# The end of the ramp: the last stage's rows in one area, loaded by six DMAs; the second batch's first product between the `pd` groups; the rounding of weights reordered

## The chip, the cores and the metric

The kernel runs on one core of one Trainium2 chip. A core has five engines that run their own streams of instructions: TensorE (PE) multiplies matrices, VectorE (DVE), ScalarE (ACT) and GpSimd (POOL) work on tensors elementwise, and SyncE (SP) issues DMAs. ScalarE and GpSimd can issue DMAs too. Engines wait for each other and for DMAs through semaphores. Operands lie in SBUF (128 partitions), products in PSUM (eight banks of 128 x 512 fp32). The metric is the time of one execution in microseconds; lower is better.

## The reference

A Fourier filter over the sequence, then a two-layer network with SiLU on every token:

```python
# x (8, 3008, 256), filt_r and filt_i (1505, 256)
X = np.fft.rfft(x, axis=1)
y = np.fft.irfft(X * (filt_r + 1j * filt_i)[None], n=x.shape[1], axis=1)
# t = y reshaped to (24064, 256); w_in (256, 2048), w_out (2048, 256)
h = t @ w_in
out = (h * (1.0 / (1.0 + np.exp(-h)))) @ w_out
```

The weights arrive as 64-bit floats; the kernel rounds them to fp32 on the chip.

## The kernel before, in words

**Two halves that interleave.** The sequence of 3008 is split as 47 x 64 (in fact 94 x 32 with real arithmetic), so that the Fourier transform becomes small matrix products. For one batch (`spectral(b)`) the stages are: a product over rows (`pa`, `stage1`), a product over the other factor (`pb`, `forward`), the multiplication with the filter (`multiply`, `add`), the inverse product (`pc`, `inverse_first` for batch 0), a pass of the rows through DRAM to change the layout (`rows_first` stores to `d2`, `load_t4` loads from it), and the last product (`pd`, `stage3`), whose result is the input `y` of the network. The network works on pairs of token blocks, 48 steps for each batch; a step (`hidden` and `project`) does seven products into `px` and `pyz`, SiLU into `g`, and seven products into `acc`, with the seven-product (Strassen-like) form of a 2 x 2 block product. That form needs sums of weight blocks, which `combine_weights(jp)` makes for pair `jp` of the eight pairs of 128-column weight blocks.

**The ramp.** Only batch 0 runs ahead of the loop; the other batches' stages are placed between the products of the loop's steps by `plan` and `put(step, round, piece)`. The order is written out by hand: the program records instructions in this order, each engine runs its own in that order, and semaphores do the rest. A piece at `put(k, 7, ...)` is recorded after the last round of step `k`. Tiles come from pools with a fixed number of buffers; asking for one more makes the writer wait for the readers of the oldest. In the ramp PSUM banks are dealt in rotation by `bank` with a counter, `early[0]`; `early[0] = None` ends that.

**The end of the ramp**, which the change touches. For groups `g` = 0 to 5 of eight rows, `inverse_first(g)` fills two banks, and `rows_first(g)` (L515 to L521) copies each to SBUF with ScalarE and stores it to `d2` in DRAM: ScalarE issues the store, but GpSimd for group 4. `rows_first` takes its two tiles from the pools `q` and `o`, two buffers each, so a copy of group 5 waits for the store of group 3. Stage 3 needs all 48 rows of `d2`, for four columns a time. `load_t4(g, first, last)` (L539 to L547) loads rows `first` to `last` of the four columns of group `g`, one DMA for each half `h`, into a tile of its own. Before the change it is called for `g` = 0 to 3 and rows 0 to 24, then 24 to 32, then 32 to 48, when the stores of these rows are on their way: 24 DMAs, of which SP issues 20 and ScalarE the four with `first == 32` and `h == 1`.

While the rows travel, the weight blocks 4 to 8 are turned into fp32: `split` (L922 to L932: VectorE takes exponent and mantissa bits apart, ScalarE turns them into floats), `rounded` (L938 to L944, VectorE) and `placed` (L953, VectorE: the product goes to its place in `w_t`). The exponent of a block goes over two ScalarE pieces (L931, L932) for the blocks 0, 2, 4 and 6 and over one VectorE piece (L940) for the others. `combine_weights` runs on VectorE for pair 0 and on GpSimd for pairs 2 and 3. TensorE runs filler products (`idle_wide`, L1015), whose result nobody reads, and then `stage3` for the groups 0 to 3, each into two banks; between groups stand filler products of 256 columns (L554). The banks are evicted into `y` in turn by VectorE (L244) and ScalarE (L246, and L576 for group 0). Then `tokens` (the `ty` tile, VectorE) starts the loop.

**The first steps of the loop.** In step 0 the second batch's first row product stands between the products of the network (`stage1(0)` of batch 1, `put` at step 0, round 3: the `pa` rows of L333), with two evictions by ScalarE (L349), and the same for `u` = 1 to 7 in steps 1 to 7. In these steps another weight block is split, rounded and placed too.

Of the kernel before, what the change touches and what calls it, by code (L numbers as in the profile page):

```python
# [167 lines left out]
def kernel(  # L168
# [51 lines left out]
    w_t = cpool.tile([128, NJP, 7, 2, 128], FP32)  # L220
    warm = cpool.tile([128, 1], FP32)
    bias_t = cpool.tile([128, 5], FP32)
    x_all = xpool.tile([128, 2, 2, 2 * C], FP32)
# [13 lines left out]

    flip, early = [0], [0]

    def evac(dst, src):  # L240

        flip[0] ^= 1
        if flip[0]:
            nc.vector.tensor_copy(out=dst, in_=src)  # L244
        else:
            nc.scalar.copy(out=dst, in_=src)  # L246

# [19 lines left out]
    def spectral(b):  # L267
# [24 lines left out]

# [27 lines left out]
        def sums(u):  # L320
# [4 lines left out]
            us[u] = ut  # L325

        def stage1(u):
            t1 = tpool.tile([128, 2, 2, C], FP32, name=f"t1_{b}_{u}", tag="t")
            ps = [bank(b, f"pa_{b}_{u}_{h}", HIDDEN[h] if b > 1 and u == 6 else None) for h in range(2)]
            if b == 1:  # L330
                xt = xs.pop(u)
                for h in range(2):
                    nc.tensor.matmul(out=ps[h].rearrange("p n c -> p (n c)"), lhsT=wx_t,  # L333
                                     rhs=xt[0:96, 512 * h:512 * h + 512], start=True, stop=True)
                if u + 2 < 8:
                    load_x(u + 2)
            else:
                ut = us.pop(u)
                for par in range(2):
                    for h in range(2):  # L340
                        rows = slice(64 * h, 64 * h + N1)
                        nc.tensor.matmul(out=ps[h][64 * par:64 * par + 64], lhsT=wf_t[rows, par],  # L342
                                         rhs=ut[rows, par], start=True, stop=True)
# [171 lines left out]
        def rows_first(g):  # L515
            for i, pool, tag in ((0, qpool, "q"), (1, opool, "o")):
                qt = pool.tile([128, 2, C], FP32, name=f"q_{b}_{g}_{i}", tag=tag)
                nc.scalar.copy(out=qt, in_=halves[g][i])
                a0 = 8 * g + 4 * i
                queue = nc.gpsimd if g == NG - 2 else nc.scalar  # L520
                queue.dma_start(out=d2[a0:a0 + 4].rearrange("a n h c -> (a n) h c"), in_=qt)  # L521

# [15 lines left out]

        def load_t4(g, first=0, last=2 * NS):  # L539
            if first == 0 and b == 0 and g in (2, 3):  # L540
                t4s[g] = tpool.tile([128, 4, C], FP32, name=f"t4_{b}_{g}", tag="t")
            elif first == 0:
                t4s[g] = t4pool.tile([128, 4, C], FP32, name=f"t4_{b}_{g}", tag="t4")
            for h in range(2):
                queue = nc.scalar if first == 32 and h == 1 else nc.sync
                queue.dma_start(out=t4s[g][64 * h + first:64 * h + last],
                                in_=d2[first:last, 4 * g:4 * g + 4, h, :])  # L547

        def stage3(g, home=None, fill=()):
# [3 lines left out]
            for moving in fill:  # L553
                nc.tensor.matmul(out=room[0][:, 0], lhsT=wx_t, rhs=moving, start=True, stop=True)  # L554
            ps = [t.rearrange("p a c -> p (a c)")[:, 0:8 * N1]
                  .rearrange("p (a i n) -> p a i n", a=2, i=4) for t in room]
            for cb in range(2):
                for i in range(4):
                    for c0 in (0, 64):
                        for h in range(2):  # L560
                            rows = slice(64 * h, 64 * h + 2 * NS)
                            nc.tensor.matmul(  # L562
                                out=ps[h][c0:c0 + 64, cb, i, :],
                                lhsT=t4s[g][rows, i, 128 * cb + c0:128 * cb + c0 + 64],
                                rhs=wi_t[rows, :], start=True, stop=True)
# [8 lines left out]
            for h in range(2):  # L574
                if g == 0:
                    nc.scalar.copy(out=dst[:, :, h, n0:n0 + 4], in_=ps[h])  # L576
                else:
                    evac(dst[:, :, h, n0:n0 + 4], ps[h])

        def evict_y(g, h):  # L580
# [4 lines left out]

        return dict(evict_y=evict_y, evict_t1=evict_t1, halves=halves, load_first=load_first, stage1_first=stage1_first, load_x=load_x, sums=sums, stage1=stage1, reverse_x=reverse_x,
                    load_fold=load_fold, fold=fold, stage1_fold=stage1_fold, evict_fold=evict_fold,
                    load_t2=load_t2, forward=forward, multiply=multiply, add=add, inverse=inverse, inverse_first=inverse_first, rows_first=rows_first, even=even, rows=rows, load_t4=load_t4, stage3=stage3)

# [319 lines left out]
    def split_weights(*js):  # L909
# [17 lines left out]
        for j in js:  # L927
            if j in (0, 2, 4, 6):

# [5 lines left out]
    def round_weights(*js):  # L935
        for j in js:
            lo, hi, e, m, ef, mf = raws[j]
            v.scalar_tensor_tensor(out=mf, in0=lo, scalar=2.0 ** -52, in1=mf, op0=ALU.mult, op1=ALU.add)  # L938
            if j not in (0, 2, 4, 6):
                v.tensor_scalar(out=e, in0=ef, scalar1=255.0, scalar2=float(1 << 23),  # L940
                                op0=ALU.min, op1=ALU.mult)
# [115 lines left out]
    for g in range(NG):  # L1057
# [10 lines left out]
        if g == 2:  # L1068
# [129 lines left out]
```

## Time and profile before

| | us |
|---|---|
| median of three runs (2581.76 to 2582.83) | 2582.73 |
| the profiled execution | 2582.95 |
| its span, first to last instruction | 2581.1 |
| TensorE busy in the span | 2560.4 |
| VectorE busy | 1679.8 |
| ScalarE busy | 1112.5 |
| GpSimd busy | 424.0 |

In the table of stages, the end of the ramp and the first steps read (busy us in the stretch, mean rate of all DMAs):

| stretch, us | what runs | TensorE | VectorE | ScalarE | GpSimd | GB/s |
|---|---|---|---|---|---|---|
| 36.0 to 62.2 | batch 0 up to the last inverse product | 25.45 | 23.33 | 13.69 | 11.51 | 280 |
| 62.2 to 72.9 | rows through DRAM, filler on TensorE | 9.50 | 10.56 | 6.34 | 4.90 | 189 |
| 72.9 to 80.2 | stage 3, groups 0 to 3, evictions | 7.30 | 5.88 | 3.91 | 3.27 | 34 |
| 80.2 to 88.0 | step 0 | 6.95 | 6.06 | 4.80 | 2.02 | 328 |
| 88.0 to 96.0 | step 1 | 8.00 | 6.25 | 4.29 | 1.97 | 191 |
| 96.0 to 104.0 | step 2 | 8.00 | 6.43 | 4.57 | 1.97 | 185 |

A line of the timeline is read as: start in us from the span's start, duration, engine, line of the kernel, operation, written tile, read tiles, shape, number of merged instructions, and in brackets how long the engine had been idle and what it had waited for. An engine name with q is its sequencer, which issues DMAs. [...] The chain that ended last is followed back from the last instruction, each step to what released it.

### The profile page before, as it was taken

To read this page: it belongs to the slowest core of one execution; us is meant where nothing else is said; L and a number is where in the kernel's file an instruction comes from. 1 tells how busy PE (TensorE), PEld (TensorE's weight loads), DVE (VectorE), ACT (ScalarE), POOL (GpSimd) and SP (SyncE) were. 2 spreads that over 40 slices of the span, in tenths; PEclk is the share of its full clock that TensorE was granted. 3 is DMA by queue.
4 is the path that set the end of the run, shared out by engine and by line. 5 is a ranking of instruction groups with operands and counts; after the bars stand their busy time and mean duration, and the time that the engine had idled before them with its cause. 6 is when DMAs were issued, how large, how long until landed. Compare 5 with 4: busy or idle time off the path is not lost.

```text
span 2581.1 us, 48332 instructions
## 1 busy us (share of the span) xinstructions
PE 2560.4 (99%) x18956; PEld 2197.1 (85%) x18956; DVE 1679.8 (65%) x3569; ACT 1112.5 (43%) x3014; POOL 424.0 (16%) x672
## 2 busy tenths in 40 slices
PE   8999999999999999999999999999999999999998
PEld 6788888888888888888888888888888888888987
DVE  7866666666666666666666666666666666555554
ACT  3544444444444444444444444444444444444443
POOL 2211111121112111311122111211121112101101
PEclk9999999999999999999999999999999999999999
DMA  8531232222222222322223122331232211200000
GB/s 279 156 74 49 72 79 63 60 63 75 60 63 69 70 62 58 77 72 66 61 65 83 50 66 58 80 80 46 66 85 64 69 42 33 58 19 16 9 17 17
DMA packets 200077, 171.08 MB, mean 66 GB/s; under 512 B 122116, under 2 KB 174196, under 8 KB 199060
## 3 DMA queue, kind: packets, MB, share of 16 engines
q1 hardware_dynamic: 178520, 117.04, 18.5%
q0 software_dynamic: 16928, 44.65, 5.4%
q10 hardware_dynamic: 4400, 6.29, 0.8%
q8 instruction: 149, 2.44, 0.4%
q14 instruction: 80, 0.66, 0.1%
HBM read 96.05 MB, written 81.26 MB: 69 GB/s over the span
## 4 chain that ended last, share of the span: by engine, by line
PE 96%; DVE 1%; DMA 1%; ACT 1%; issue 0%; ACTq 0%; POOL 0%; SPq 0%; DVEq 0%; POOLq 0%
PE acc L797 43%; PE px L734 25%; PE pyz L734 19%; PE pd L562 3%; PE pb L446 2%; PE pc L489 2%; PE pf L416 1%; DMA filt<-in_filt_r_dram 1%; DVE g L705 0%; DMA w_t<-in_x_dram 0%; PE pa L342 0%; PE pc L511 0%; PE idle L1015 0%; ACT t L349 0%; ACTq L233 0%
## 5 line engine op out<-in xcount | busy, mean ns | idle before, releaser
L797 PE MATMUL acc<-g,w_t 128*128 128x256 f32 (+1 forms) x5376 | 1509.1, 375 | 0.4 <-DVE g L705 0.4
L797 PEld LDWEIGHTS acc<-g,w_t 128*128 128x128 f32 x5376 | 1021.8, 190 | 115.2 <-DVE g L705 0.8
L705 DVE TENSOR_TENSOR g<-pyz,abc 128x256 f32<-128x256 f32 (+1 forms) x1152 | 479.3, 416 | 613.4 <-ACT abc L755 359.6
L705 DVE TENSOR_TENSOR g<-g 128x256 f32<-128x256 f32 (+3 forms) x1152 | 598.2, 519 | 196.5 <-ACT g L738 183.4
L734 PE MATMUL px<-ty,w_t 128*128 128x256 f32 (+1 forms) x2304 | 677.9, 376 | 0.7 <-ACT abc L755 0.6
L738 ACT ACTIVATE g<-g 128x256 f32<-128x256 f32 (+1 forms) x1152 | 472.9, 410 | 250.0 <-DVE g L705 250.0
L734 PEld LDWEIGHTS px<-ty,w_t 128*128 128x128 f32 x2304 | 432.3, 190 | 64.4 <-issue 7.9
L705 POOL TENSOR_TENSOR s<-s 128x256 f32<-128x256 f32 (+1 forms) x329 | 254.7, 791 | 1412.9 <-DVE s L817 1307.8
L734 PE MATMUL pyz<-y,w_t 128*128 128x256 f32 (+1 forms) x1536 | 453.8, 377 | 0.0
L734 PEld LDWEIGHTS pyz<-y,w_t 128*128 128x128 f32 x1536 | 283.2, 189 | 48.1 <-DVE g L705 8.9
L749 ACT COPY abc<-px 128x256 f32<-128x256 f32 (+1 forms) x384 | 141.1, 368 | 365.2 <-PE px L734 365.2
L755 ACT COPY abc<-px 128x256 f32<-128x256 f32 (+1 forms) x384 | 141.6, 369 | 336.3 <-PE px L734 335.6
L738 ACT ACTIVATE g<-px 128x256 f32<-128x256 f32 (+1 forms) x384 | 145.8, 380 | 297.6 <-PE px L734 297.5
L734 PE MATMUL px<-y,w_t 128*128 128x256 f32 (+1 forms) x768 | 231.9, 384 | 0.1
L734 PE MATMUL pyz<-ty,w_t 128*128 128x256 f32 (+1 forms) x768 | 225.3, 375 | 0.2 <-DVE g L705 0.2
L734 PEld LDWEIGHTS px<-y,w_t 128*128 128x128 f32 x768 | 140.0, 189 | 33.2 <-DVE y L584 5.8
L734 PEld LDWEIGHTS pyz<-ty,w_t 128*128 128x128 f32 x768 | 144.3, 190 | 18.8 <-DVE g L705 1.0
L742 ACT COPY abc<-px 128x256 f32<-128x256 f32 (+1 forms) x384 | 135.4, 353 | 43.7 <-PE px L734 43.7
L562 PEld LDWEIGHTS pd<-wi_t,t 48*64 48x64 f32 x4096 | 65.7, 135 | 28.8 <-ACT g L738 16.4
L428 POOL DMA_DIRECT2D d<-tf x144 | 71.4, 503 | 29.5 <-DVE tf L424 25.4
L817 ACT COPY s<-acc 128x512 f32<-128x512 f32 (+1 forms) x94 | 54.2, 577 | 47.6 <-PE acc L797 47.5
L562 PE MATMUL pd<-wi_t,t 48*64 48x47 f32 x4096 | 72.2, 233 | 2.5 <-issue 2.2
(124 smaller groups left out, 1316.0 us busy)
## 6 DMA issues: line engine op xcount, KB each, us to landing
t<-d SPq DMA_DIRECT2D x120, 192.0 KB
d<-q POOLq DMA_DIRECT2D x86, 256.0 KB, 2.6
t<-d SPq DMA_DIRECT2D x84, 256.0 KB
out_dram<-o SPq DMA_DIRECT2D x636, 32.0 KB
d<-tf POOLq DMA_DIRECT2D x144, 96.0 KB, 3.2
xr<-in_x_dram SPq DMA_DIRECT2D x6, 1472.0 KB
x_all<-in_x_dram SPq DMA_DIRECT2D x72, 96.0 KB
x_all<-xr SPq DMA_DIRECT2D x72, 96.0 KB
```

The lines of the kernel that those rows point to most:

```text
L428: nc.gpsimd.dma_start(out=d1[k // 2, :, k % 2, n0:n0 + 4], in_=us["tf"][32 * k:32 * k + NS].rearrange("p q n c -> p (q n) c"))
L446: nc.tensor.matmul(out=ps[k][32 * j:32 * j + 32, ri, :], lhsT=d_t[rows, 4 * g + at, ri, :], rhs=t2[rows, at, :], start=True, stop=True)
L489: nc.tensor.matmul(out=ps[j][64 * k:64 * k + 64, a, :], lhsT=e_t[rows, g + a, k, ri, :], rhs=zs[k][rows, ri, :], start=(a == 0 and ri == 0 ...
L562: nc.tensor.matmul(out=ps[h][c0:c0 + 64, cb, i, :], lhsT=t4s[g][rows, i, 128 * cb + c0:128 * cb + c0 + 64], rhs=wi_t[rows, :], start=True, ...
L705: eng.tensor_tensor(out=out, in0=in0, in1=in1, op=op)
L734: nc.tensor.matmul(out=out, lhsT=w_t[:, jp, c, 0], rhs=rhs, start=start, stop=True, skip_group_check=True)
L738: nc.scalar.activation(out=g[:, k, 0:n], in_=g[:, k, 0:n] if src is None else src, func=AFT.Silu)
L742: nc.scalar.copy(out=sums[:, 0, 0:n], in_=xo)
L749: nc.scalar.copy(out=sums[:, 1, 0:n], in_=xo)
L755: nc.scalar.copy(out=sums[:, 2, 0:n], in_=xo)
L797: nc.tensor.matmul(out=acc[pair][i][:, h, 0:n], lhsT=w_t[:, jp, c, 1], rhs=g[:, k, 0:n], start=(jp == 0 and h == 0), stop=last, skip_group ...
L817: copy(out=s[:, 2 * i:2 * i + 2, 0:n], in_=acc[pair][i][:, :, 0:n])
```

## The change

The rows of stage 3 for groups 0 to 3 no longer lie in four tiles. They lie in one area of `w_t`, `us["t4"]`, in the part that holds the weight pairs 5 to 7 later and the input of the forward products earlier. `load_t4_rows(first, last)` loads rows for all sixteen columns with one DMA per half, from SP: rows 0 to 24 (recorded after the last `forward` now, at `g == 3`, with the second batch's first rows and weight block 9 behind it), 24 to 32, and 32 to 48, six DMAs instead of 24. All stores of rows are issued by ScalarE; the second copy of the last group (5) is VectorE's. Between the `pd` groups 0, 1 and 2 stand the two halves of the second batch's first product (512 columns each) instead of filler products of 256; `stage1(0)` in step 0 then only evicts. The filler ahead of stage 3 is ten wide and twelve narrow products instead of 21 wide ones, in a bank of its own name. Of the `pd` evictions, VectorE takes the second ones of groups 2 and 3, ScalarE all others. The exponent of block 4 takes the VectorE piece. The combination of pair 2 is done by VectorE, half of it at the end of step 0 and half at the end of step 1; that of pair 3 stays on GpSimd, behind a one-column copy (`gate`) that reads what the last `placed` wrote.

```diff
+    gate = cpool.tile([128, 1], FP32)
@@ load_first
             us["t2"] = view[:, 6144:14336].rearrange("p (s c) -> p s c", c=C)
+            us["t4"] = view[:, 8960:13056].rearrange("p (n c) -> p n c", c=C)
@@ stage1
+        def rows_product(u, h, ps=None):
+            if ps is None:
+                ps = bank(b, f"pa_{b}_{u}_{h}")
+                us.setdefault("rows", []).append(ps)
+            nc.tensor.matmul(out=ps.rearrange("p n c -> p (n c)"), lhsT=wx_t,
+                             rhs=xs[u][0:96, 512 * h:512 * h + 512], start=True, stop=True)
...
-                xt = xs.pop(u)
-                for h in range(2):
-                    nc.tensor.matmul(out=ps[h].rearrange("p n c -> p (n c)"), lhsT=wx_t,
-                                     rhs=xt[0:96, 512 * h:512 * h + 512], start=True, stop=True)
+                if u > 0:
+                    for h in range(2):
+                        rows_product(u, h, ps[h])
+                else:
+                    ps = us["rows"]
+                xs.pop(u)
@@ rows_first
-                nc.scalar.copy(out=qt, in_=halves[g][i])
+                copy = nc.vector.tensor_copy if g == NG - 1 and i == 1 else nc.scalar.copy
+                copy(out=qt, in_=halves[g][i])
                 a0 = 8 * g + 4 * i
-                queue = nc.gpsimd if g == NG - 2 else nc.scalar
-                queue.dma_start(out=d2[a0:a0 + 4].rearrange("a n h c -> (a n) h c"), in_=qt)
+                nc.scalar.dma_start(out=d2[a0:a0 + 4].rearrange("a n h c -> (a n) h c"), in_=qt)
@@ load_t4
-            for h in range(2):
-                queue = nc.scalar if first == 32 and h == 1 else nc.sync
-                queue.dma_start(out=t4s[g][64 * h + first:64 * h + last],
-                                in_=d2[first:last, 4 * g:4 * g + 4, h, :])
+        def load_t4_rows(first, last):
+            for h in range(2):
+                nc.sync.dma_start(out=us["t4"][64 * h + first:64 * h + last], in_=d2[first:last, 0:16, h, :])
@@ stage3
-                if g == 0:
-                    nc.scalar.copy(out=dst[:, :, h, n0:n0 + 4], in_=ps[h])
-                else:
-                    evac(dst[:, :, h, n0:n0 + 4], ps[h])
+                copy = nc.vector.tensor_copy if g > 1 and h == 1 else nc.scalar.copy
+                copy(out=dst[:, :, h, n0:n0 + 4], in_=ps[h])
@@ split_weights, round_weights
-            if j in (0, 2, 4, 6):
+            if j in (0, 2, 6):
@@ the ramp
             part["rows_first"](2)
-            for later in range(4):
-                part["load_t4"](later, 0, 24)
+        if g == 3:
+            part["load_t4_rows"](0, 24)
             second["load_x"](0)
             weights(9)
...
     part["rows_first"](3)
-    for later in range(4):
-        part["load_t4"](later, 24, 32)
     split(4, 5)
     combine_weights(0)
-    for g in (4, 5):
-        part["rows_first"](g)
+    part["rows_first"](4)
+    part["load_t4_rows"](24, 32)
     rounded(4, 5)
+    part["rows_first"](5)
+    part["load_t4_rows"](32, 2 * NS)
     placed(4, 5)
     split(6, 7, 8)
-    combine_weights(2, eng=gp)
-    for g in range(4):
-        part["load_t4"](g, 32, 2 * NS)
     rounded(6, 7)
     placed(6, 7)
-    combine_weights(3, eng=gp)
     rounded(8)
     placed(8)
-    idle_wide(21)
+    gp.tensor_copy(out=gate, in_=w_t[:, 4, A11, 0, 0:1])
+    combine_weights(3, eng=gp)
+    stand = bank(0, "stand")
+    idle_wide(10, stand)
+    idle(12, stand)
...
     for g in range(4):
-        part["stage3"](g, fill=((), (wide_rows,), (wide_rows,), (last_x,))[g])
+        early[0] = 1 if g in (0, 3) else early[0]
+        part["stage3"](g, fill=(last_x,) if g == 3 else ())
+        if g < 2:
+            second["rows_product"](0, g)
...
+    for k in range(2):
+        put(k, 7, combine_weights, 2, k)
```

More of the change, by code (lines that the diff above doesn't have):

```diff
@@ L236, in load_filters @@
                                     ap=[[94 * C, 16], [t * C, last - first], [1, C]]))
[L238 to L244, printed above, removed]
-        else:
-            nc.scalar.copy(out=dst, in_=src)
+    early = [0]
     y = {}
@@ L325, in sums @@
             us[u] = ut
+        def rows_product(u, h, ps=None):
[4 more added lines that the diff above has]
+                             rhs=xs[u][0:96, 512 * h:512 * h + 512], start=True, stop=True)
         def stage1(u):
             t1 = tpool.tile([128, 2, 2, C], FP32, name=f"t1_{b}_{u}", tag="t")
-            ps = [bank(b, f"pa_{b}_{u}_{h}", HIDDEN[h] if b > 1 and u == 6 else None) for h in range(2)]
+            ps = None
+            if b > 1 or u > 0:
+                ps = [bank(b, f"pa_{b}_{u}_{h}", HIDDEN[h] if b > 1 and u == 6 else None) for h in range(2)]
             if b == 1:
-                xt = xs.pop(u)
-                for h in range(2):
-                    nc.tensor.matmul(out=ps[h].rearrange("p n c -> p (n c)"), lhsT=wx_t,
-                                     rhs=xt[0:96, 512 * h:512 * h + 512], start=True, stop=True)
+                if u > 0:
[4 more added lines that the diff above has]
+                xs.pop(u)
                 if u + 2 < 8:
@@ L537, in rows, with load_t4 @@
                 nc.gpsimd.dma_start(out=d2[a0:a0 + 4].rearrange("a n h c -> (a n) h c"), in_=qt[:, a])
[L539 to L543, printed above, removed]
+        def load_t4(g):
+            t4s[g] = t4pool.tile([128, 4, C], FP32, name=f"t4_{b}_{g}", tag="t4")
             for h in range(2):
-                queue = nc.scalar if first == 32 and h == 1 else nc.sync
-                queue.dma_start(out=t4s[g][64 * h + first:64 * h + last],
-                                in_=d2[first:last, 4 * g:4 * g + 4, h, :])
+                nc.sync.dma_start(out=t4s[g][64 * h:64 * h + 2 * NS], in_=d2[:, 4 * g:4 * g + 4, h, :])
+        def load_t4_rows(first, last):
+            for h in range(2):
+                nc.sync.dma_start(out=us["t4"][64 * h + first:64 * h + last], in_=d2[first:last, 0:16, h, :])
         def stage3(g, home=None, fill=()):
@@ L556, in stage3 @@
                   .rearrange("p (a i n) -> p a i n", a=2, i=4) for t in room]
+            t4 = us["t4"][:, 4 * g:4 * g + 4] if b == 0 and g < 4 else t4s[g]
             for cb in range(2):
@@ L563, in stage3 @@
                                 out=ps[h][c0:c0 + 64, cb, i, :],
-                                lhsT=t4s[g][rows, i, 128 * cb + c0:128 * cb + c0 + 64],
+                                lhsT=t4[rows, i, 128 * cb + c0:128 * cb + c0 + 64],
                                 rhs=wi_t[rows, :], start=True, stop=True)
@@ L574, in stage3 @@
             for h in range(2):
-                if g == 0:
-                    nc.scalar.copy(out=dst[:, :, h, n0:n0 + 4], in_=ps[h])
-                else:
-                    evac(dst[:, :, h, n0:n0 + 4], ps[h])
+                copy = nc.vector.tensor_copy if g > 1 and h == 1 else nc.scalar.copy
+                copy(out=dst[:, :, h, n0:n0 + 4], in_=ps[h])
         def evict_y(g, h):
@@ L584, in evict_y @@
             copy(out=dst[:, :, h, n0:n0 + 4], in_=us["pd", g][h])
-        return dict(evict_y=evict_y, evict_t1=evict_t1, halves=halves, load_first=load_first, stage1_first=stage1_first, load_x=load_x, sums=sums, stage1=stage1, reverse_x=reverse_x,
+        return dict(evict_y=evict_y, evict_t1=evict_t1, halves=halves, load_first=load_first, stage1_first=stage1_first, load_x=load_x, rows_product=rows_product, sums=sums, stage1=stage1, reverse_x=reverse_x,
                     load_fold=load_fold, fold=fold, stage1_fold=stage1_fold, evict_fold=evict_fold,
-                    load_t2=load_t2, forward=forward, multiply=multiply, add=add, inverse=inverse, inverse_first=inverse_first, rows_first=rows_first, even=even, rows=rows, load_t4=load_t4, stage3=stage3)
+                    load_t2=load_t2, forward=forward, multiply=multiply, add=add, inverse=inverse, inverse_first=inverse_first, rows_first=rows_first, even=even, rows=rows, load_t4=load_t4, load_t4_rows=load_t4_rows, stage3=stage3)
     pending = []
@@ L938, in round_weights @@
             v.scalar_tensor_tensor(out=mf, in0=lo, scalar=2.0 ** -52, in1=mf, op0=ALU.mult, op1=ALU.add)
-            if j not in (0, 2, 4, 6):
+            if j not in (0, 2, 6):
                 v.tensor_scalar(out=e, in0=ef, scalar1=255.0, scalar2=float(1 << 23),
```

## The prediction

> **What bounds the kernel now.** I read the page's first part, then the chain that ended last between 60 and 82 us, then the timeline around it, because the diff touches only what lies between the last inverse product and the second step of the main loop.
>
> ```profile
> span 2581.1 us, 48332 instructions
> PE 2560.4 (99%) x18956; PEld 2197.1 (85%) x18956; DVE 1679.8 (65%) x3569; ACT 1112.5 (43%) x3014; POOL 424.0 (16%) x672
> ```
>
> TensorE is busy for 99% of the span, but in the ramp part of that is filler (`idle`). From about 80 us on, the loop runs as one body that the diff leaves alone except for two small pieces; so what moves the loop's start, or stretches its first steps, moves the end by as much. The chain in the window:
>
> ```profile
> 62.19 9.26 PE idle L1015 x42
> 71.45 0.24 PE pd L562 x2
> 71.70 1.21 issue
> 72.90 1.14 PE pd L562 x62
> 74.04 0.63 PE pd L554 x2
> ...
> 79.35 0.82 ACT y L246
> 80.16 0.04 issue
> 80.21 0.70 DVE ty L705
> ```
>
> TensorE has nothing useful to do from 62.2 to 72.9 us: 21 filler products, then 1.21 us of waiting for a load. Stage 3 (`pd`) truly starts at 72.90, ends at 79.35, and two evictions later (80.21) the loop begins. Why so late, from the timeline (start, duration, engine; q marks a DMA issue):
>
> ```profile
> 62.23 0.59 ACT L518 COPY q<-pc 128x512 f32<-128x512 f32 x1 [0.21 <-PE pc L511]
> 62.84 0.33 ACTq L521 DMA_DIRECT2D d<-q  x1
> 62.95 6.58 SPq L546 DMA_DIRECT2D t<-d  x12
> 63.26 0.58 ACT L518 COPY q<-pc 128x512 f32<-128x512 f32 x1 [0.45 <-DMA d<-q]
> 63.88 0.33 ACTq L521 DMA_DIRECT2D d<-q  x1
> 69.44 1.88 ACTq L546 DMA_DIRECT2D t<-d  x4
> ```
>
> The last store of rows goes out at 63.88. SP's last four loads start at 67.83 (found in a narrower window), after 0.5 us of waiting for that store, so it landed at about 67.75: 3.9 us after issue. The other four loads sit in ScalarE's queue behind the rounding and go out from 69.44. The first of them is what `pd` of group 0 waits for: 72.87 - 69.44 = 3.4 us from issue to use.
>
> [...] no line of this trace shows the engines, but I credit the wider loads with no better spread. [...] VectorE's 0.42 us rounding pieces take 0.95 us while GpSimd combines (63.62 to 67.07 us).
>
> **The change, part by part.**
>
> Loads before the last rows. Eight loads of 24 rows (3.24 us of SP issue from 53.09) become two; at 0.4 each SP is free 2.4 us sooner. They now overwrite an area that the last forward product reads, which ends at 51.7, before the stores they wait for anyway (53.09): cost nothing. The batch-two rows and a weight pair follow sooner. DMA was saturated from 55.5 to 62.5 us and the third group's store, issued at 56.93, landed only at 62.95; with the backlog started earlier I estimate 61. The two loads of rows 24 to 31 follow it, eight before; they are out by 62, while SP's next wait ends at 66, so they cost nothing unless that store lands after 65.
>
> Last stores. Two ScalarE pieces for block 4 go (0.71 + 0.72); VectorE does 0.42 instead, inside its 0.43 us wait from 59.27. Group 4's stores move from GpSimd (issued 61.84) to ScalarE (about 60.2 and 61.2): two issues of 0.33 and the copies fit before the last inverse product ends at 62.19; if they did not, up to 0.7 us would show. Group 5's second copy goes to VectorE at 62.2 to 62.9, beside ScalarE's, so its store goes out at 63.2 instead of 63.88: 0.7 gained. ScalarE's issue waits there for VectorE; behind it stands only a rounding piece that needs VectorE's next result. The store took 3.9 us under load, GpSimd's two just before it 3.1 in the list of DMA issues, and the one issued at 50.52, in a quiet moment, 2.5 (SP waited for it until 53.05); with less queued, I take 2.9: landed at 66.1. Ends: 65.7 (2.5) and 67.1 (3.9).
>
> Last loads. Two of SP, 256 KB each, in place of eight of 64 KB from two queues. The second is issued at 66.1 + 0.4 = 66.5 and needs 3.4 us as before: **stage 3 starts at 69.9**. Group 0 now needs all sixteen columns, not four; the bytes are the same 512 KB, 1.9 us at the 280 GB/s that the stretch from 36 to 62 us moved, and I count them inside the 3.4. Ends: 69.5, where the filler stops (20 wide passes of 0.22 and 24 narrow ones of 0.124 after 62.12), and 71.9 if store and loads both keep the long times (67.1 + 0.4 + 3.4 + 1.0 for the larger pieces). Gain 72.90 - 69.9 = **+3.0** (1.0 to 3.4).
>
> Products between `pd` groups. Two separators of 256 columns become the two halves of the second batch's first product, 512 columns: in `pa` rows four passes take 1.72, so 0.86 each instead of 0.43. **-0.86**. The 1.72 they leave in step 0 are worth nothing: there ScalarE sets the pace.
>
> ```profile
> 82.52 0.72 ACT L924 ACTIVATE e<-e,bias_t 128x512 f32<-128x512 uint32 x1 [1.19 <-DVE e L922]
> 83.15 0.61 ACT L926 ACTIVATE m<-m 128x512 f32<-128x512 uint32 x1
> 83.67 0.35 ACT L749 COPY abc<-px 128x256 f32<-128x256 f32 x1
> ...
> 84.23 1.06 ACT L349 COPY t<-pa 128x512 f32<-128x512 f32 x2
> 85.18 0.39 ACT L755 COPY abc<-px 128x256 f32<-128x256 f32 x1
> 85.62 0.70 PE L734 MATMUL px<-ty,w_t 128*128 128x256 f32 x2 [0.56 <-ACT abc L755]
> ```
>
> ScalarE works without a break from 82.52 to 85.57 and TensorE waits for it at the end; none of these pieces goes.
>
> Evictions of `pd`: ScalarE gets four in a row, 0.75 each, against 2.1 us from group to group; the last pair is still one on each engine. Nothing. VectorE no longer meets GpSimd in the rounding and ends it near 73.8 (76.5 before), ahead of its first eviction near 75.5; the gate holds GpSimd's combination to 74 to 77, before `ty` at 78. If that slipped, a `ty` piece would double: 0.4.
>
> Combination of pair 2. Four operations leave GpSimd and stand in VectorE's queue at the end of steps 0 and 1, ahead of the addition that frees `pyz`.
>
> ```profile
> 88.53 0.42 DVE L705 TENSOR_TENSOR g<-pyz,abc 128x256 f32<-128x256 f32 x1
> 92.81 0.38 ACT L755 COPY abc<-px 128x256 f32<-128x256 f32 x1
> 93.43 0.59 PE L734 MATMUL px<-ty,w_t 128*128 128x256 f32 x2
> 93.57 0.87 DVE L705 TENSOR_TENSOR w_t<-w_t 128x256 f32<-128x256 f32 x2
> 96.53 0.42 DVE L705 TENSOR_TENSOR g<-pyz,abc 128x256 f32<-128x256 f32 x1
> ```
>
> The same pair of operations occupies VectorE for 0.79 (93.57 to the next start at 94.36); its second kind for 0.67. At 88.53 there are 0.2 us of slack, so VectorE, and ScalarE's rounding behind it, run 0.58 late; TensorE had 0.24 between the copy's end (93.19) and its product (93.43): 0.4 lost. In step 1 there is no slack (95.93 + 0.60 = 96.53): 0.58 + 0.67 = 1.25 late, and in step 2 TensorE already waited for that copy. **-1.2** in all (0 if hidden, 1.5 if fully added).
>
> Sum: 3.0 - 0.9 - 1.2 = +0.9 us. The profiled execution took 2582.95 us (span 2581.1); it would take 2582.0. The runs' median is 2582.73, so **2581.8**.
>
> **Rivals.** *The two combinations are absorbed*: VectorE is 65% busy, so the steps may take them in. For: steps 1 and 2 have gaps on VectorE. Against: those lie after the rounding that ScalarE waits for. Then +2.1: 2580.6. *The wide loads come late, and it gets slower*: 256 KB pieces, needed whole before group 0, behind a store that lands as late as now. For: DMA is still loaded at 63 to 67 us. Against: half of the backlog is gone and issuing no longer paces the loads. Stage 3 at 71.9: 1.0 - 0.9 - 1.2 = -1.1, 2583.8. It decides from a start later than 70.8. *The change doesn't do what it says*: what it saves on queues becomes waiting for the same store, start near 70.8, 2582.7.
>
> **How the numbers follow.** Mine 0.5, absorbed 0.2, late loads 0.2, no gain 0.1. Forecast 2581.8; with mine alone 2581.0 to 2582.6. Leaving a tenth at each end and allowing for the runs' own spread (1.07 us): 2580.2 to 2583.7. A measurement can tell about 0.2% from no change, 5.2 us here; no case moves more than 2.2 us, and the whole wait before stage 3 is 10.7 us of which most is a real round trip. So 0.96 for within 0.2%, and 0.02 each side for what I don't see.
>
> **What would show it.** Right: last store issued near 63.2; six loads of rows, the last two from SP near 66; `pd` from 69.5 to 70.5; two `pa` pairs of 0.86 between groups; `ty` near 78.1; step 0 as long as before although it has no `pa`; TensorE gaps behind ScalarE's copies in steps 1 and 2, about 1.2 us in sum. Wrong: `pd` after 71, or no loss in steps 1 and 2, or a loop whose later steps change their length.

## The result: slower by 14 us, and the profile after

The changed kernel takes 2596.98 us (median of four runs, 2596.37 to 2597.97) against 2582.78 of the kernel before (four runs, 2581.76 to 2583.27): ratio 1.0056, 95% interval 1.0038 to 1.0073. The forecast was 2581.8 with a range of 2580.2 to 2583.7. The profiled execution took 2596.74 us. The head of its page:

```profile
span 2595.0 us, 48298 instructions
PE 2566.1 (99%) x18954; PEld 2199.1 (85%) x18954; DVE 1679.7 (65%) x3574; ACT 1112.2 (43%) x3012; POOL 419.8 (16%) x667
```

VectorE and ScalarE were busy for as long as before, GpSimd for 4.2 us less. TensorE is 5.7 us *busier* although its filler was cut: a first hint that its products ran longer. The chain that ended last, in the stretch that the prediction speaks of (start, duration, what):

```profile
61.86 3.73 issue
65.59 0.70 DVE q L524
66.30 0.02 issue
66.32 5.93 DMA d<-q
...
72.37 0.31 SPq L551
72.68 0.04 issue
72.72 5.97 DMA w_t<-d
78.69 0.14 issue
78.82 1.95 PE pd L567 x62
80.77 2.00 PE pa L325 x2
82.78 1.89 PE pd L567 x64
...
91.60 2.00 PE idle L1018 x4
93.60 0.85 PE px L737 x2
```

The last inverse product ends at 61.86, 0.3 us sooner than before. Then TensorE does next to nothing useful for 17 us. The path goes over VectorE's copy of the last rows, which starts only at 65.59, its store (5.93 us) and the last loads (5.97 us). Stage 3 starts at 78.82 in place of 72.90. And it is slow: a `pd` group takes 1.89 us (1.08 to 1.17 before), a half of the row product 2.00 where I forecast 0.86. From the start of stage 3 to the first product of the loop it takes 14.6 us (the timeline has that product at 93.40), 7.35 before (80.25 - 72.90).

Why the copy waits, from the timeline of ScalarE, VectorE and TensorE:

```profile
55.54 0.33 ACTq L526 DMA_DIRECT2D d<-q  x1
56.58 0.33 ACTq L526 DMA_DIRECT2D d<-q  x1
62.18 0.33 ACTq L526 DMA_DIRECT2D d<-q  x1
63.94 0.59 ACT L524 COPY q<-pc 128x512 f32<-128x512 f32 x1 [3.10 <-DMA d<-q]
65.59 0.69 DVE L524 COPY q<-pc 128x512 f32<-128x512 f32 x1 [3.88 <-issue]
66.14 2.84 PE L1012 MATMUL stand<-wx_t 96*128 96x128 f32 x24
77.00 0.42 PE L567 MATMUL pd<-wi_t,w_t 48*64 48x47 f32 x2 [8.02 <-DMA w_t<-d]
78.82 1.95 PE L567 MATMUL pd<-wi_t,w_t 48*64 48x47 f32 x62 [1.40 <-DMA w_t<-d]
```

Group 5's copies write the tiles that group 3's stores read. These stores, issued at 55.54 and 56.58, let ScalarE copy at 63.94 and VectorE at 65.59, 8.4 and 9.0 us later. (That VectorE waited for the second store is inferred: the line names "issue", but the semaphore events of the trace have that store landing at 65.51.) TensorE's filler ends at 69.0, and TensorE stands still for 8.0 us. (A product stands in the trace as two records: the twelve narrow ones are the `x24` of L1012.)

The windows, after first and before second (busy us; PEclk is the granted TensorE clock):

```profile
62.20:72.90 10.70, 6.78 (x44) 6.10 (x42) 6.37 (x16) 5.43 (x9) 0.00 (x0) 0.92 0.67 206
72.90:80.20 7.30, 1.79 (x54) 1.70 (x58) 4.52 (x10) 0.00 (x0) 2.88 (x5) 0.50 0.54 74
80.20:88.00 7.80, 7.80 (x141) 4.61 (x138) 0.00 (x0) 2.84 (x4) 0.21 (x1) 0.50 0.01 2
```

```profile
72.90:80.20 7.30, 7.30 (x264) 5.75 (x264) 5.88 (x7) 3.91 (x5) 3.27 (x4) 1.00 0.15 34
```

The clock was 1.00 before and is 0.50 here. By finer windows it falls at 71.2, 2.2 us after the filler's end, and is back at 95.1: the whole of stage 3 and the start of step 0 run at half speed.

The two profiled spans differ by 13.9 us (the medians by 14.2): 5.9 (78.82 - 72.90) from a later start, 7.2 (14.6 - 7.35) from a longer stage 3, of which about 0.86 is the wider products and so some 6.4 the clock, and the remaining 0.8 from what follows. The experiments ask two things: what makes stores and loads late, and what lowers the clock.

### The profile page after: what moved, and what is told of

The parts are those of the page before. It is cut to its first block, busy times and chain, and to the rows that moved or that the text cites. A ratio compares the mean times of both kernels' runs of the same rounds, so it can differ in the third digit from the quotient of the medians.

```text
span 2595.0 us, 48298 instructions
## 1 busy us (share of the span) xinstructions
PE 2566.1 (99%) x18954; PEld 2199.1 (85%) x18954; DVE 1679.7 (65%) x3574; ACT 1112.2 (43%) x3012; POOL 419.8 (16%) x667
## 4 chain that ended last, share of the span: by engine, by line
PE 95%; DMA 2%; DVE 1%; ACT 1%; issue 0%; SPq 0%; ACTq 0%; DVEq 0%
PE acc L800 43%; PE px L737 25%; PE pyz L737 19%; PE pd L567 3%; PE pb L451 2%; PE pc L494 2%; PE pf L421 1%; DMA filt<-in_filt_r_dram 1%; DVE g L708 0%; DMA w_t<-in_x_dram 0%; PE pa L347 0%; PE pc L516 0%; PE pa L325 0%; DMA w_t<-d 0%; DMA d<-q 0%
## 5 line engine op out<-in xcount | busy, mean ns | idle before, releaser
L850 DVE STREAM_TRANSPOSE o<-s 128x256 f32<-128x256 f32 x192 | 74.0, 423 | 0.7 <-issue 0.7
```

Source lines behind the costliest of these rows:

```text
L850: v.transpose(out=o[:, :, h, :], in_=results[pair][:, ((2, 6), (4, 1))[chunk][h], :])
```

## The experiments

Theory L (loads): a whole 16-column load writes one narrow stretch of partitions (24, 8 or 16 neighbouring ones of one half), and one half comes after the other; such loads are slow. This was my conjecture: the trace of the changed kernel shows only how long they take (5.97 us for the last pair, from the issue of the second). The small loads of the kernel before alternate halves, so by the theory both halves take in data at once. Theory C (clock): TensorE's idle time ahead of `pd` lowers the clock. Rivals: the filler's narrow products lower it, or the lateness as such; and for the loads, the length of the contiguous runs that a DMA is made of (1 KB each, however the loads are cut) or the backlog in general.

Single runs unless said otherwise; the kernel before took 2581.6 to 2582.7 beside them.

### A longer filler

```diff
-    idle_wide(10, stand)
+    idle_wide(28, stand)
```

> The changed kernel with 28 wide filler products instead of 10 ahead of stage 3, so that TensorE has work until about 77 us instead of 69. Theory 'cold clock': the stage 3 groups took 1.89 us instead of 1.1, and the products between them 2.00 instead of 0.86, because TensorE stood idle for 8 us and its clock was granted at 0.5; with the filler the clock stays at 1.0, stage 3 still starts near 78.8, lasts about 8 us instead of 14.6, and the time falls by 6 to 6.5 us, to about 2590.6. Rival 'the operands are slow': the groups are slow because they read their rows from the area of w_t while GpSimd and the DMAs work there; then the groups stay at 1.9 us and the time at 2597.

2599.67 us. The filler now ended at 78.1 and `pd`'s operands came at 79.80, after a pause of 1.31 us. The clock was 1.00 until 80.3 and then 0.50. A miss: an almost full filler did not hold the clock. The pause was about that of the kernel before (1.21), whose clock held in its profile. Either narrow products count as little work, or 1.2 us is at the edge.

### All loads in four-column pieces, halves alternating

```diff
-            for h in range(2):
-                nc.sync.dma_start(out=us["t4"][64 * h + first:64 * h + last], in_=d2[first:last, 0:16, h, :])
+            for c in range(0, 16, 4):
+                for h in range(2):
+                    nc.sync.dma_start(out=us["t4"][64 * h + first:64 * h + last, c:c + 4],
+                                      in_=d2[first:last, c:c + 4, h, :])
```

> The changed kernel with each of its six loads cut in four (four columns each), the two halves taking turns, all from SP, into the same area. Theory 'narrow door': the rows of one half lie in 24, 8 or 16 neighbouring partitions[...]. Then [...] the third group's stores land near 62 instead of 63.9 and 65.6, stage 3 starts at 72 to 74 and the time is 2583 to 2588. Rival 'runs of 1 KB': each run costs the same 0.12 us on its engine however the loads are cut; then the rates stay, stage 3 starts at 78 or later, and the time stays at 2597 or grows by SP's additional issues (18 of 0.4 us).

2590.72 us. The chain:

```profile
69.03 1.79 issue
70.82 0.40 PE pd L569 x2
...
75.22 1.89 PE pd L569 x64
```

`pd` started at 70.82, earlier than in the kernel before (72.90), with the same bytes, area and queue: the size and order of the loads are the whole lateness. I expected 72 to 74. Yet the time is 8 us above the goal and outside the 2583 to 2588 that I expected, since the clock fell to 0.5 at 70.8, after a pause of 1.8 us; the `pd` groups took 1.89 us. The two causes come apart. (The chain also has a later wait here, 3.79 us for a weight load in step 0.)

### The last loads on every fourth partition, and on two queues

```diff
-                nc.sync.dma_start(out=us["t4"][64 * h + first:64 * h + last], in_=d2[first:last, 0:16, h, :])
+                rows = slice(64 * h, 64 * h + 64, 4) if first == 32 else slice(64 * h + first, 64 * h + last)
+                nc.sync.dma_start(out=us["t4"][rows], in_=d2[first:last, 0:16, h, :])
```

These are 16 partitions of a half again, but spread over all 64.

> The changed kernel with the last two loads (rows 32 to 48) written to every fourth partition of their half instead of 16 neighbouring ones: same source, bytes, runs, queue and number of DMAs, other partitions. The rows of stage 3 are then not in their place, so the output is not the reference's. Theory 'narrow door': [...] from the issue of the first of them to the start of stage 3 it takes 3.9 us instead of 6.4, and the time falls by 2.4 us or more. Rival 'runs of 1 KB': the same 6.4 us and the same time, 2597.

2594.19 us. The loads' part of the chain:

```profile
71.33 0.62 SPq L552
71.95 0.05 issue
72.00 3.88 DMA w_t<-d
```

3.88 us against 5.97 with the same bytes, count and runs, on every fourth partition: 2.1 us less (1.8 from the issue of the first load, where I expected 2.5). The length of the runs is excluded as the cause. How the partitions are spread limits these loads; by what means, no run shows.

A second queue for the second half, which needs no smaller pieces to have both halves in flight:

```diff
-                nc.sync.dma_start(out=us["t4"][...], in_=d2[first:last, 0:16, h, :])
+                (nc.sync, nc.gpsimd)[h].dma_start(out=us["t4"][...], in_=d2[first:last, 0:16, h, :])
```

> The changed kernel with the second half's three loads issued by GpSimd, which has nothing else to do there, instead of SP; sizes and places stay. Theory 'narrow door': [...] the last loads land about 2 us earlier after their issue, the first ones by 62 us or before, stage 3 starts at 72 to 75 and the time is 2583 to 2590. Rival 'the halves serialize anyway', whichever queue issues: the same 6 us for the last loads, and a time of 2595 or more.

2594.54 us. The last store went out at 65.04 and needed 4.41 us, but the last load 5.82 us from its issue by GpSimd. A second queue for the second half gains earlier stores and nothing for the last loads, so the expected 72 to 75 missed (`pd` started at 76.04). So two large loads onto two halves took as long from two queues as from one (5.82 us and 5.97).

### Which loads delay what

Only one group of loads is cut into the pieces above, or the first two. The edit for rows 0 to 24 is shown in part; the others put `first == 32`, `first == 24` and `first < 32` in the condition.

```diff
+            cut = 4 if first == 0 else 16
+            for c in range(0, 16, cut):
```

> The changed kernel with only the loads of rows 0 to 24 cut into four-column pieces of alternating halves. If those long loads delay the third group's stores, and these the copies of the sixth, then the last store is issued about 2 us sooner than in the changed kernel (near 64.3) and lands near 69, the last two loads still need about 6 us, and pd starts at about 75.5: 3 us shorter than the changed kernel, about 2594. If the first loads have nothing to do with it, no change.

> The changed kernel with only the loads of rows 32 to 48 cut into four-column pieces of alternating halves. [...] both halves at a time take them 6.0 -> 3.5 us and pd has its last operands at about 76.3 in place of 78.8, the time is about 2.4 us shorter, near 2594.4; the last store still lands near 72.2. If it is the engines' backlog, the loads still land near 78.8.

> The changed kernel with only the loads of rows 24 to 32 cut into four-column pieces of alternating halves. If these two loads (128 KB a half into 8 partitions) hold the engines that the last store needs, the store lands 1.5 to 3 us after its issue sooner than now: issue still near 66.3, landing near 69 to 70 in place of 72.3, pd near 76 and the time near 2594. If it is the first loads' backlog, it lands near 72 again and the time is unchanged.

> The changed kernel with the loads of rows 0 to 24 and of rows 24 to 32 cut, those of rows 32 to 48 whole. If the two groups of loads delay the stores together, the last store is issued near 64.5 and lands near 67.5 to 69, the last two loads still need about 6 us, pd has its operands at 74 to 75.5 and the time is 2592 to 2593.5. If the store still lands at 72, the loads of the rows are not what holds it.

The last inverse product itself ends up to 1.5 us sooner or later from profile to profile (the first filler product starts at 61.7 to 63.3), so the start of stage 3 is also counted from there:

| loads cut | filler starts | last store issued | landed after | last loads, DMA | `pd` from | from filler's start | time |
|---|---|---|---|---|---|---|---|
| none (changed kernel) | 61.72 | 66.32 | 5.93 | 5.97 | 78.82 | 17.1 | 2596.98 |
| rows 0 to 24 | 62.67 | 64.57 | 7.84 | 6.04 | 78.99 | 16.3 | 2597.30 |
| rows 24 to 32 | 62.16 | 65.81 | 3.64 | 5.87 | 75.88 | 13.7 | 2594.74 |
| both | 63.00 | 64.95 | 3.46 | 6.03 | 75.01 | 12.0 | 2592.76 |
| rows 32 to 48 | 63.27 | 67.97 | 5.88 | 2.10 (first piece) | 76.32 | 13.0 | 2594.76 |
| kernel before | 62.12 | 63.88 | 3.9 | | 72.90 | 10.8 | 2582.78 |

The chain of the kernel with rows 0 to 24 cut, then of the one with rows 24 to 32 cut:

```profile
62.83 0.07 DVE q L524
...
64.57 7.84 DMA d<-q
...
72.81 6.04 DMA w_t<-d
```

```profile
65.09 0.70 DVE q L524
...
65.81 3.64 DMA d<-q
...
69.88 5.87 DMA w_t<-d
```

My expectation for the first missed: VectorE's copy of group 5 came at 62.83, as soon as its product was there, in place of 65.59, as said, but the store landed at 72.4 all the same. The second shows why: the two loads of rows 24 to 32, 128 KB each, hold the store; cut, the store needs 2.3 us less from its issue. (Each is a single profile.) Counted from the filler's start, the first loads alone give 0.8 us, the middle ones 3.4, both together 5.1. The last loads cut give 4.1 us.

What is gained by the last loads is order, not rate. By the semaphore events of the traces, the two large ones had both landed 6.3 us after the first was issued (72.37 to 78.69). The eight pieces had all landed after 6.2 us (73.97 to 80.12), and those of the kernel before after 6.4 (67.83 to 74.21). But the first piece was there after 2.1 us, and group 0 needs only the first two. That is the pipelining that the sixteen-column load took away. My 76.3 for `pd` came true (76.32), but for this reason and not for the one I gave. So theory L holds in part: the spread over partitions limits a large load, but for the last loads no run shows that taking turns makes the whole faster. What pieces did change besides, in the two groups ahead, is the wait of the stores.

### What lowers the clock

```diff
-    idle_wide(10, stand)
+    idle_wide(34, stand)
```

> The changed kernel with 34 wide products ahead of the 12 narrow ones in place of 10, so that the filler ends after the last loads have landed and TensorE never stands still. If an idle TensorE is what lowers the clock, pd starts right behind the filler at about 79.7, its groups take 1.1 us and the first px comes about 8.4 us later: about 2591.5. If the narrow products by themselves lower it, or the late operands do, the groups take 1.9 us and the time is 2598 or more.

2591.73 us, where I expected 2591.5. The chain:

```profile
62.35 14.87 PE stand L1018 x68
77.22 2.69 PE stand L1012 x24
79.91 0.04 issue
79.96 1.25 PE pd L567 x64
81.20 1.05 PE pa L325 x2
82.26 1.08 PE pd L567 x64
```

Though stage 3 starts at 79.96, 1.1 us later than in the changed kernel, the whole is 5 us faster: no pause, full clock (1.00 from 72.9 to 88.0), `pd` 1.08 and the product halves 1.05. From the start of stage 3 to the end it takes 2510.0 us, against 2516.2 in the changed kernel: 6.1 us, near the 6.4 put down to the clock above. Twelve narrow products did no harm. (A half's 1.05 stands against a separator's 0.63: +0.42, so two cost +0.84, as forecast.)

The kernel before with the changed filler:

```diff
-    idle_wide(21)
+    stand = bank(0, "stand")
+    idle_wide(10, stand)
+    idle(12, stand)
```

> The kernel before with the changed kernel's filler: 10 wide and 12 narrow products in place of 21 wide ones, its loads and all else as before. If the filler's kind and early end let the clock fall, the clock drops to 0.5 at about 71, stage 3 takes about 13 us in place of 7.35 and the time is near 2588.5. If the clock in the changed kernel fell only because its operands came so late, the kernel before keeps its clock and its 2582.7.

2589.88 us, +7.3. The timeline of TensorE:

```profile
67.07 2.84 PE L1009 MATMUL stand<-wx_t 96*128 96x128 f32 x24
70.93 0.28 PE L562 MATMUL pd<-wi_t,t 48*64 48x47 f32 x2 [1.02 <-DMA t<-d]
73.81 1.95 PE L562 MATMUL pd<-wi_t,t 48*64 48x47 f32 x62 [2.60 <-DMA t<-d]
```

Pauses of 1.02 and 2.60 us, and the clock falls (its mean is 0.55 from 72.9 to 80.0, and 0.50 from 80.0 to 88.0) though the loads are the old ones. So the filler cut alone makes half of the loss in this run. Whether narrow filler or the pause does it:

```diff
-    idle_wide(21)
+    idle_wide(24)
```

> The kernel before with 24 wide products of filler in place of 21, so that the filler reaches to the operands. If a pause ahead of pd is what lowers the clock, and 12 of 39 runs of the kernel before lost 4 to 7 us to it (mean clock 0.995 to 0.997), no run of this kernel does: all stay within 2580 to 2584, with stage 3 starting at 73.0 to 73.2 (0.1 to 0.3 later than in the kernel before). If those runs have another cause, about a third of these runs take 2586 to 2589 too.

```diff
-    idle_wide(21)
+    idle_wide(18)
```

> The kernel before with 18 wide products of filler in place of 21: the pause ahead of pd grows from 1.2 to about 2.5 us. If the pause alone decides, the clock falls in most runs and the median is 2586 to 2589. If the narrow products of the changed filler count as little work, so that the light stretch must exceed about 2.7 us (12 narrow ones ran without harm when pd followed at once), the clock holds as often as in the kernel before and the median stays within 0.5 us of it.

With 24: median 2581.96 of 12 runs, 2581.16 to 2584.34; ratio 0.9993, interval 0.9984 to 1.0001. With 18: median 2588.53, 19 of 20 runs between 2586.75 and 2589.99, one at 2580.47; ratio 1.0017, interval 1.0010 to 1.0023. The windows of the profile with 18, all its filler wide:

```profile
66.00:70.20 4.20, 4.20 (x20) 3.37 (x18) 4.09 (x8) 3.62 (x6) 1.11 (x2) 1.00 0.40 134
70.20:74.20 4.00, 2.13 (x75) 1.66 (x77) 3.93 (x8) 0.66 (x2) 1.75 (x2) 1.00 0.64 102
74.20:87.80 13.60, 13.60 (x209) 10.39 (x209) 7.24 (x12) 4.77 (x9) 2.09 (x3) 0.50 0.51 158
```

There are two waits of 0.49 and 1.38 us before `pd` (1.9 in all, not the 2.5 expected), which then starts at full clock, and at 74.2 the clock falls for 13.6 us of uninterrupted work. The pause is enough; narrow filler is not needed for it. The kernel before stands at the edge: of the 70 runs of it made beside the repeated kernels, 20 took 2585.7 to 2589.9 us, 19 of them at a mean clock of 0.997 or less (of the other 50 only four), while the 12 with 24 products had none. There is no trace of such a run; that they are the same fall is an inference from size and clock.

The traces show more. All changes of the clock in one profile lie whole multiples of 3.41 us apart (the fall in the changed kernel lasts 23.89 us, seven of them, the one in the kernel with 18 lasts 13.65, four), so each profile can be cut into windows of this length. Here is the window just ahead of the fall in the changed kernel, in the one with the longer filler and in the one with 18, and last the window with the pause of the kernel before, which kept its clock (the number behind the comma is TensorE's busy time):

```profile
67.81:71.22 3.41, 1.17 (x11) 0.98 (x9) 3.24 (x9) 3.23 (x6) 0.00 (x0) 1.00 0.52 87
76.92:80.33 3.41, 2.04 (x50) 1.76 (x51) 1.41 (x3) 0.00 (x0) 2.16 (x4) 1.00 0.35 35
70.82:74.23 3.41, 2.03 (x78) 1.55 (x77) 3.38 (x7) 0.69 (x2) 1.78 (x2) 1.00 0.61 80
70.14:73.55 3.41, 2.21 (x54) 1.68 (x53) 3.38 (x7) 0.00 (x0) 1.14 (x2) 1.00 0.52 96
```

TensorE is busy for 0.34, 0.60 and 0.60 of the first three and for 0.65 of the last. In the eighteen profiles, from 37 to 115 us, there are 17 falls, each right behind a window busy for 0.60 or less. None follows a window above that, though five at 0.56 to 0.60 stayed without a fall. So by these traces what counts is how much of one window is idle, and a pause of 1.2 to 1.3 us is at the edge: 1.21 us in one window left 0.65, 1.31 us left 0.60. Where a window begins differs from profile to profile, and a pause may be split between two, which would make the fall a matter of chance near the edge. No run moved the pause against the windows to test it.

The way back is as plain. All 17 falls ended behind a window at least 0.87 busy in which products of a step (`px`, `pyz`) ran. As long as `pd` products ran, windows filled to 1.00 left the clock at 0.50. So a fall just ahead of stage 3 costs all of stage 3.

### Both repaired, and the two other steps

Quarter loads with 21 wide products, no narrow ones:

```diff
-    idle_wide(10, stand)
-    idle(12, stand)
+    idle_wide(21, stand)
```

> The changed kernel with the quarter loads of the run with four-column pieces (halves alternating, all on SP) and with the wide filler of the kernel before (21 wide products, no narrow ones). If the remaining loss of the quarter run is the clock, which fell because the filler ended in narrow products [...], the filler now ends near 70.8, stage 3 starts at about 71.3, the clock stays at 1.0 through it, pd groups take 1.1 us, the wide product pairs 0.86, and the kernel ends at 2582.2 to 2583.5: 72.90 - 71.3 = -1.6 for the start, +0.86 for the wider products, +1.2 for the combination of pair 2 in the stages' steps, against the kernel before. If the clock falls anyway (a cause other than the filler's kind), pd groups take 1.9 us and the time stays near the quarter run's 2590.7.

On top of it, the combination of pair 2 back on GpSimd; the row product back in step 0 and the separators back (`stage1(0)` then makes the products again, which is not shown); both:

```diff
+    combine_weights(2, eng=gp)
     combine_weights(3, eng=gp)
-    for k in range(2):
-        put(k, 7, combine_weights, 2, k)
```

```diff
-        part["stage3"](g, fill=(last_x,) if g == 3 else ())
-        if g < 2:
-            second["rows_product"](0, g)
+        part["stage3"](g, fill=((), (wide_rows,), (wide_rows,), (last_x,))[g])
```

> The kernel with quarters and wide filler, with the combination of pair 2 given back to GpSimd, behind the gate and ahead of that of pair 3. If those two VectorE combinations at the ends of steps 0 and 1 cost what I put on them, this is 1.2 us (0 to 1.5) shorter than the kernel with quarters and wide filler; if the combinations are absorbed by slack there, the same within 0.3 us.

> The kernel with quarters and wide filler, with the second batch's first product back in step 0 and the wide separators (0.43 us each) back between the first three pd groups. If the product costs 2 x (0.86 - 0.43) on the path and its absence from step 0 is worth nothing, this is 0.86 us shorter than the kernel with quarters and wide filler; if step 0 gains by the absence, the same or longer.

> Both of the last two edits together, on quarters and wide filler: only the loads, the stores' queues and the roundings differ from the kernel before. If the terms add up, 2.06 us shorter than the kernel with quarters and wide filler and about 1.6 us shorter than the kernel before, near 2581.0 (2580.0 to 2582.0). If the combinations and products overlap with other slack, between 2581 and 2583.

| kernel (12 runs each) | median | range | ratio, interval | span less start of stage 3 |
|---|---|---|---|---|
| quarters, wide filler | 2583.65 | 2582.33 to 2584.20 | 0.9997 (0.9988 to 1.0005) | 2510.6 |
| the first, with pair 2 on GpSimd | 2583.68 | 2581.56 to 2584.16 | 0.9998 (0.9989 to 1.0006) | 2510.3 |
| the first, with the product in step 0 | 2582.97 | 2581.81 to 2592.86 | 1.0000 (0.9990 to 1.0010) | 2508.9 |
| the first, with both | 2582.58 | 2579.90 to 2583.65 | 0.9997 (0.9989 to 1.0006) | 2508.6 |

Four-column loads and a filler that reaches to `pd` take back 13.3 of the 14.2 us, and with both steps undone all of it: stage 3 starts right behind the filler (at 71.82 in the first) at full clock (1.00 from 77 to 84 in its windows, its `pd` groups 1.08 to 1.25 us). By the ratios none of these four can be told from the kernel before (median 2582.62 of 39 runs). But 12 of those 39 took 2585.7 or more; the other 27 have a median of 2581.86, and the four lie 0.7 to 1.8 us above it. So the stage 3 that starts sooner did not make a kernel that is faster than an undisturbed run of the kernel before, and I had expected 2581.0 of the last.

Between the four the differences are near the spread, so only a tendency: the row product in step 0 against between the groups, 1.7 us in the profiles, 0.7 and 1.1 in the medians; the combination, 0.3 in the profiles and 0.0 and 0.4 in the medians. I expected 0.86 and 1.2.

The difference for the row product is more than the two products' extra width, and the windows show what else. With the product between the groups, then with it in step 0:

```profile
80.00:84.00 4.00, 2.65 (x10) 1.38 (x9) 2.92 (x7) 2.02 (x5) 0.00 (x0) 1.00 1.01 335
84.00:88.00 4.00, 3.48 (x8) 2.10 (x9) 2.86 (x7) 2.09 (x6) 2.22 (x4) 0.52 1.01 330
```

```profile
80.00:84.00 4.00, 3.52 (x10) 1.73 (x10) 2.99 (x7) 2.89 (x7) 0.00 (x0) 1.00 1.04 334
84.00:88.00 4.00, 3.68 (x16) 2.79 (x16) 3.31 (x9) 1.53 (x5) 2.21 (x4) 1.00 1.06 342
```

Without the product TensorE is busy for 2.65 of 4 us in step 0 and the clock falls again, for two windows (6.8 us). All three profiles with the product moved and stage 3 at full clock have such a fall in step 0 (6.8, 3.4 and, in the changed kernel with 34 wide products, 3.4 us); none of the four with the product in step 0 and an undisturbed stage 3 has it.

The version with both undone has the lowest median of the four, and the kernel before with 24 products is as good with one number changed. In a typical run neither beats the kernel before measurably; what they spare is the runs at 2586 and above, of which 24 runs of these two had none. The version with only the product moved back had one at 2592.86, at a mean clock of 0.995. It has no pause ahead of `pd` in its profile, and there is no trace of that run, so its cause is open.

## Why the prediction was wrong

**Last stores: failed.** I wrote that "with the backlog started earlier I estimate 61" for the third group's store. (What I called saturated, 55.5 to 62.5 us before, had the DMA engines busy for 0.88 of the time.) It landed at 65.51, behind the two large first loads, and held VectorE's copy to 65.59; with the first loads in pieces the copy came at 62.83. The last store was issued at 66.32, not 63.2 (+3.1), and needed 5.93 us, not 2.9 (+3.0). I kept open that the loads of rows 24 to 32 cost nothing "unless that store lands after 65"; it did, and they then stood ahead of the last store: cut, 3.64 us.

**Last loads: failed.** "I credit the wider loads with no better spread" asked only whether they gain. The 3.4 us from issue to use was the time of one 64 KB piece. The trace of the kernel before already had all eight pieces landing 6.4 us after the first was issued, but there group 0 had its four columns early. The sixteen-column load took that head start away, so `pd` now waits for the whole. That "the bytes are the same 512 KB" and fit inside the 3.4 used 280 GB/s, the mean rate of all DMAs from 36 to 62 us. From the store's landing to `pd` it took 6.6 us, not 3.8 (+2.8). Together 8.9 us: 78.82 in place of 69.9.

**The rival** "the wide loads come late, and it gets slower" had the mechanism and the side, but it was sized at 71.9 for stage 3 and had a chance of 0.2; its start was off by 7 us because I let store and loads at most keep their old durations.

**Missing term: the clock.** I noted that the filler "stops" at 69.5 and read it as the earliest start for `pd`, a gain. That it also kept the clock up had no place in the sum. It cost about 6.4 us of the 14, and by the runs it would have cost them even with loads on time: the quarter run started stage 3 at 70.8, about where I forecast it, and took 2590.72. That "no case moves more than 2.2 us" therefore failed on this side too: the pause of 1.21 us in the profile before was already an exposure, and I took the shorter filler without asking what it was for.

**Products between groups:** -0.86 was right at full clock (0.42 each, as 1.05 against 0.63; I had written 0.86 against 0.43). But "the 1.72 they leave in step 0 are worth nothing" was too kind: the profiles with the product moved show a further fall of the clock there, to 0.50 for 3.4 to 6.8 us.

**Combination of pair 2:** -1.2 is not confirmed; the pair of runs without and with it differ by 0.0 and 0.4 us, so the rival "absorbed" was nearer. **Rounding and evictions:** VectorE's and ScalarE's totals are unchanged, and none of their pieces stood on the path ahead of stage 3 except the copy at 65.59.

## What to carry to other kernels

Fewer and larger DMAs are not cheaper by themselves: ask how the partitions that one of them writes are spread (5.97 us for two onto 16 neighbouring ones, 3.88 onto every fourth of 64), what is on its way beside it, stores from other queues too (5.93 us beside two whole loads, 3.64 beside eight pieces), and whether its first reader needed only a part of it (the first of eight pieces landed after 2.1 us). In this kernel filler on TensorE is part of the clock (`pd` groups of 1.08 us at 1.00 with filler up to `pd`, of 1.89 us at 0.50 behind a pause of 8.0): before it is cut, or a pause before real work grows by a microsecond, count the half-speed time behind it, and see whether the kernel is already at the edge by looking at all its runs, not only at the one profiled.

## What was not expected of the hardware

- A pause of 1.2 us ahead of `pd` let the clock fall in perhaps 20 of 70 runs and 1.9 us (in two parts) in 19 of 20; without a pause it fell in none of 12. The fall comes at the end of a 3.41 us window in which TensorE was busy for 0.60 or less (17 of 17 falls; none behind a window at 0.65), so it can come after work has resumed.
- Ahead of stage 3 it stays at 0.50 for 13.6 to 23.9 us, through the rest of `pd`, though windows are filled to 1.00; it came back only behind a window of step products.
- 256 KB in two loads onto eight partitions each made a store on another queue take 2.3 us longer (5.93 against 3.64) than the same bytes in eight loads of alternating halves.
- 512 KB in two loads took 5.97 us onto 16 adjacent partitions of each half and 3.88 us onto every fourth of 64, from the issue of the second. In eight pieces of 64 KB, 16 adjacent partitions again, all had landed no sooner (6.2 us after the first issue against 6.3), but the first did after 2.1 us.
